# Two half heads instead of one pair: exponentials of an attention kernel split between ScalarE and VectorE

## The chip, the cores and the metric

One core of one Trainium2 chip. The metric is the device time of one execution in microseconds (us), the median of the runs shown. Lower is better.

## The reference, cut to what matters

Two attention layers over 2048 tokens of width 576 with 32 heads of 18 channels each; their outputs stand side by side. A has one key and one value head for all query heads (softmax over all 2048 keys). B has its own keys and values per head, works in four segments of 512 tokens with a causal mask, and adds a memory of the earlier segments.

```python
def _A_ref(x, wq, wk, wv, wo):
    q = (x @ wq).reshape(B, S, H, Dh).transpose(0, 2, 1, 3)
    k, v = x @ wk, x @ wv
    p = _softmax(jnp.einsum("bhqd,bkd->bhqk", q, k) * (Dh ** -0.5), axis=-1)
    return jnp.einsum("bhqk,bkd->bhqd", p, v) ... @ wo

def _B_ref(x, wq, wk, wv, wo, beta):
    for s in range(N):
        p = _softmax(jnp.einsum("bhqd,bhkd->bhqk", qs, ks) * scale + mask, axis=-1)
        a_dot = jnp.einsum("bhqk,bhkd->bhqd", p, vs)
        o = g * a_mem + (1.0 - g) * a_dot
    ...
return jnp.concatenate([a, b], axis=-1)
```

## The kernel before

**Stages.** The first 290 us or so project x into queries, keys and values and write them to DRAM. Then comes one long loop, written out by hand, that makes scores, exponentials and products of A and B; a short tail of some 40 us projects the last chunks of A. The change is in the loop.

**Blocks, items and turns.** A block of A is a chunk of 512 queries (c, 0 to 3) and a group of four heads (hg, 0 to 7), so there are 32 of them; a block of B is a segment and a group of heads. B's 32 blocks go two at a time between blocks of A. A block of A has 16 key tiles (kt) with two pairs of heads (pr) each. One item is one key tile and one pair: a score tile E of 128 keys x (2 heads x 512 queries). The 32 items of a block are taken three at a time, as ten turns of three and an eleventh of two; they are called turn 0 to turn 10 of the block here. A block of B has six items, in two turns.

**What a turn does**, in this program order:

- `scores` (L903 and on): TensorE writes the three score tiles E into PSUM, which has three such buffers (`psE`, two banks each).
- The middle item (`copied`, i == 1) is copied by VectorE from PSUM to a tile W in SBUF (L933); with that its buffer is free.
- ScalarE takes the exponential of the three (L936), first of items 0 and 2 straight from E, then of the middle one from W, into tiles P.
- `run_fill`: four matmuls of an output projection that is ready (L773), so that TensorE has work; at its fifth step VectorE copies the result out (osb, L797).
- `products` of the turn two before (L966), six halves of items cut into turns of their own by the list `prods`. Each half serves the four heads of the group, in fp32; in the trace an entry of three halves shows as 24 matmuls, one of two as 16. The entry of two, the short turn of products, stands third from the end of a block's entries, so it is made in the block's turn 10. When a block ends, VectorE copies its sums O out (oe, L975).
- `due`: steps from a list with due turns: loads, the inverses of the softmax sums (reciprocals, L729), and the weighing of the heads by them on GpSimd (`weigh`, L754 to L764, instructions of L761). Weighing steps cost 1 each and at most two are given out in a turn, none near a B turn (`heavy`).

TensorE, ScalarE and VectorE keep this order exactly; GpSimd keeps the order of its weighing steps among each other.

**VectorE's own exponential.** One item of each block of A, key tile 0 of pair 1 (`BY_DVE = ((0, 1),)`), is not given to ScalarE. It is item 1 of turn 0, so the middle one. `exponentials` (L888) reads its E once (a scaled integer form, L894) into a tile PD of 128 x 1024, and then six further steps on SBUF tiles follow, one each in turns 0, 2, 3, 4, 5 and 6: two bitwise ones (L896, L897) and four that multiply a polynomial (L898 to L901, `scalar_tensor_tensor` with two tensor inputs). A step's due turn is the turn of the scores plus two and more, but a step goes out as soon as no block ends in the turn; so each but the first in a block goes out a turn before it is due. `LATE = (12,)` puts the products with PD at position 12 of that pair's key tiles.

Of the kernel before, what the change touches and what calls it, by code (L numbers as in the profile page):

```python
# [8 lines left out]
F32 = mybir.dt.float32  # L9
# [3 lines left out]
U32 = mybir.dt.uint32  # L13
AF = mybir.ActivationFunctionType
# [14 lines left out]
SCALE = DH ** -0.5  # L29
# [3 lines left out]
PBUFS = 9  # L33
# [18 lines left out]
POLY = [1.0925606709321247, 32.334180715292455, 88.7610992882796, 4291.093056129828]  # L52
MANTISSA, ONE_BITS, EXPONENT = 0x7FFFFF, 0x3F800000, 0xFF800000

BY_DVE = ((0, 1),)
LATE = (12,)
QALL = [(slice(0, 36, 2), 0), (slice(1, 36, 2), 1), (slice(36, 54), 0)]
CA = 618
MZ = 126 + 32
# [15 lines left out]
def attention_pair_kernel(ctx, tc, a_xT, a_w, a_wo, b_xT, b_w, b_wo, b_beta, ident_d, hmask_d, bmask_d, cmask_d, sel_d, zmask_d, selx_d, sely_d, out):  # L75
    nc = tc.nc
# [79 lines left out]
    with ExitStack() as ph:  # L156
# [106 lines left out]
        for c in range(NCH):  # L263
# [34 lines left out]
            for t in TILES:  # L298
# [3 lines left out]
                else:  # L302

                    nm, bufs = ("nd", 2) if c == 1 and t == 4 else ("pj", 4)
# [25 lines left out]
                i = 5 * (c - 2) + TILES.index(t)  # L330
# [74 lines left out]
        for s in range(NSEG):  # L405
# [110 lines left out]
            if not last:  # L516
                e = p2.tile([128, 4, DH], F32, name="ph31")
# [92 lines left out]
    with tc.If(loose > 0, preferred_fallthrough_block=False):  # L610
        with ExitStack() as ph:
# [37 lines left out]
            with tc.For_i(0, H, 1) as h:  # L649
# [5 lines left out]
                for i in range(NKT):  # L655
                    s, j = divmod(i, 4)
                    n = 128 * (j + 1)
# [17 lines left out]
    pp = ctx.enter_context(tc.tile_pool(name="pp", bufs=1))  # L675
# [79 lines left out]
    def weigh(ab, c, t, tiles):  # L755

        o, (rb, *mem) = parts[ab, c][: RT[t], t], [x[: RT[t]] for x in tiles]

        def step(dst, a, b, op):

            return lambda: tc.keep_in_program_order(nc.gpsimd.tensor_tensor(dst, a, b, op=op))  # L761

        steps = [step(o, o, rb, ALU.mult)]
        if mem:  # L764
            nb, rb2 = mem
            steps += [step(nb, nb, rb2, ALU.mult), step(o, o, nb, ALU.add)]
        return steps
# [117 lines left out]
        vseg[s] = v  # L885


    slow, now = [], [0]  # L888

    def exponentials(p, e):  # L890

        y, u, w = p.bitcast(U32), pp.tile([128, 2, 512], F32, name="n", bufs=1), pp.tile([128, 2, 512], F32, name="q", bufs=1)
        v, stt = nc.vector, nc.vector.scalar_tensor_tensor
        v.tensor_scalar(y, e, EXP_A, EXP_B, op0=ALU.mult, op1=ALU.add)  # L894
        steps = [
            lambda: v.tensor_scalar(u.bitcast(U32), y, MANTISSA, ONE_BITS, op0=ALU.bitwise_and, op1=ALU.bitwise_or),  # L896
            lambda: v.tensor_scalar(w.bitcast(U32), y, EXPONENT, None, op0=ALU.bitwise_and),  # L897
            lambda: stt(p, u, POLY[0], u, op0=ALU.add, op1=ALU.mult),  # L898
            lambda: stt(p, p, POLY[1], u, op0=ALU.add, op1=ALU.mult),
            lambda: stt(p, p, POLY[2], p, op0=ALU.add, op1=ALU.mult),  # L900
            lambda: stt(p, p, POLY[3], w, op0=ALU.add, op1=ALU.mult),  # L901
        ]
        slow.extend((now[0] + 2 + i, p, step) for i, step in enumerate(steps))  # L903

    def scores(it, pr, copied):

        ab, c, hg, kt = it
        st = stacks[ab, c, hg // 2]
        h = 2 * (hg % 2) + pr
        e = psE.tile([128, 2, 512], F32, name="E")  # L910
        dve = ab == "A" and (kt, pr) in BY_DVE
        p = pp.tile([128, 2, 512], F32, name="PD" if dve else "P", bufs=1 if dve else PBUFS)
        state[it, pr] = p
        n = 512 if ab == "A" else 512 - 128 * kt if kt < 2 else 384
        if ab == "A":
            for j, r0 in enumerate(HALF):
                rows = slice(r0, r0 + KR)
                nc.tensor.matmul(e[:, j], kstA[rows, 128 * kt : 128 * kt + 128], st[rows, h, :], start=True, stop=True)  # L918
            if (kt, pr) in BY_DVE:
                exponentials(p, e)  # L920
                return lambda: None
        else:
            for k, c0 in BKEYS[kt]:
                ks = slice(128 * k, 128 * k + 128)
                for j, r0 in enumerate(HALF):
                    rows = slice(r0, r0 + KR)
                    nc.tensor.matmul(  # L927
                        e[:, j, c0 : c0 + 512 - 128 * k], st[rows, 4 + h, ks], st[rows, h, 128 * k :], start=True, stop=True
                    )
        src = e  # L930
        if copied:
            src = pp.tile([128, 2, 512], F32, name="W", bufs=2)
            nc.vector.tensor_copy(src[:, :, :n], e[:, :, :n])  # L933

        def exponential():
            nc.scalar.activation(p[:, :, :n], src[:, :, :n], AF.Exp, scale=SCALE)  # L936
            if ab == "B":

                m = len(BKEYS[kt])
                diag = p.rearrange("p a (b t) -> p a b t", t=256)[:, :, 0:m, 0:128]  # L940
                nc.gpsimd.affine_select(  # L941
                    diag, diag, pattern=[[0, 2], [0, m], [1, 128]], base=0, channel_multiplier=-1, compare_op=ALU.is_ge, fill=0.0
                )

        return exponential
# [3 lines left out]
    def products(b, m, hf):  # L949


        ab, c, hg = b
        if m == hf == 0:
            acc[0] = psO.tile([128, C], F32, name="O")
        o = acc[0]
        last = (NKT - 1 if ab == "A" else 2) == m
        for j in range(4):
            kt = turn_of[j // 2][m] if ab == "A" else m
            p = state[b + (kt,), j // 2]
            assert all(x[1] is not p for x in slow)  # L960
            k, p0, q0, n = (kt, 256 * hf, 256 * hf, 256) if ab == "A" else BHALF[kt][hf]
            if ab == "A":
                v = VA[:, VW * kt : VW * kt + 32]
            else:
                v = vseg[c][:, k, VW * (4 * hg + j) : VW * (4 * hg + j) + 32]
            nc.tensor.matmul(  # L966
                o[32 * j : 32 * j + 32, q0 : q0 + n],
                v,
                p[:, j % 2, p0 : p0 + n],
                start=m == hf == 0,  # L970
                stop=last and hf == 1,
            )
        if last and hf:
            osb = pa.tile([128, C], F32, name="oe", bufs=4)
            nc.vector.tensor_copy(osb, o)  # L975
            od = oA if ab == "A" else oB
            nc.sync.dma_start(od[c][4 * hg : 4 * hg + 4].rearrange("h r t -> (h r) t"), osb)
            return hg
        return None
# [27 lines left out]
    turns, prods = [], []  # L1007
# [5 lines left out]
    def due(k, most=2, heavy=2):  # L1013

        cost = 0

        near = [its[n][0] for t in turns[k : k + 3] for n, pr in t]
        heavy *= "B" not in near
        for e in [e for e in later if e[0] <= k]:
            if most and cost + e[1] <= heavy and e[2]():  # L1020
                later.remove(e)
                e[3](k)
                cost += e[1]
                most -= 1
        return cost
# [60 lines left out]
    with tc.manual_schedule(engines={ENG.PE, ENG.Activation, ENG.DVE}):  # L1086
# [3 lines left out]
        for n, b in enumerate(blocks):  # L1090
            ms = [m for m in range(len(its)) if block_of[m] == n]
            items = [(m, k) for m in ms for k in range(2)]
            for out_, cut in ((turns, len(items) // 3), (prods, len(items) // 3 - 2)):
                at_ = split(len(items), cut)
                out_ += [items[a:z] for a, z in zip(at_, at_[1:])]
        at(ASK + 4, 0, lambda: True, lambda k: load_qf(2))
# [13 lines left out]
        for k in range(len(turns) + 2):  # L1110
            now[0] = k
            exps = [scores(its[n], pr, i == 1) for i, (n, pr) in enumerate(turns[k])] if k < len(turns) else []
            for i in (0, 2, 1) if len(exps) == 3 else range(len(exps)):
                exps[i]()
            if memory is None:
                run_fill()
            elif k >= ASK and all(its[n][0] == "A" for n, pr in turns[k]) and next(memory, None) is None:
                memory = None

            ends = k > 1 and any(hf and its[n][3] == (NKT - 1 if its[n][0] == "A" else 2) for n, hf in prods[k - 2])  # L1120
            if slow and (slow[0][0] <= k or not ends):
                slow.pop(0)[2]()
            for n, hf in prods[k - 2] if k > 1 else []:
                ab, c = its[n][:2]
                hg = products(its[n][:3], its[n][3], hf)
                if hg in (6, 7):
                    finish(k, ab, c, hg)
                if hg == 7 and ab == "B" and c + 1 < NSEG:
                    load_vseg(c + 1)
            due(k)  # L1130
            if k == len(turns):
                halve_w(0)
            for n, pr in turns[k] if k < len(turns) else []:
                it = its[n]
                ab = it[0]
                if pr == 0:
                    prefetch(ab, keys[ab].index((ab, it[1], it[2] // 2)) + 2)
                    if it in (("A", 0, 2, 8), ("A", 0, 5, 8)):
                        load_wo(*(("B", b_wo) if it[2] == 2 else ("A", a_wo)))
# [122 lines left out]
```

## Time and profile before

| | us |
|---|---|
| median of 3 runs (lowest to highest) | 1421.66 (1420.84 to 1422.12) |
| profiled execution: time / its span | 1422.47 / 1420.7 |
| busy in the span: TensorE matmul / weight load | 1404.0 / 843.3 |
| busy in the span: ScalarE / VectorE / GpSimd | 1205.4 / 964.4 / 244.6 |
| granted TensorE clock, mean | 0.997 |

Instructions of one engine overlap in the profile: a ScalarE or VectorE instruction starts before the one ahead of it has ended, so durations can't be added up. What an engine needs for an instruction is read from end to end of successive ones. Matmuls overlap in the same way; their rate is read from start to start.

### The profile page before, as it was taken

What the parts mean: (1) busy time and instruction counts of PE and PEld (TensorE: products, weight loads), DVE (VectorE), ACT (ScalarE), POOL (GpSimd) and SP (SyncE); (2) the same over time, 40 slices, a digit from 0 to 9 for tenths busy, and PEclk for the clock granted to TensorE, in tenths of its full rate; (3) what the DMA queues carried; (4) which work ended last, traced back from release to release, by engine and by line L of the source; (5) the groups of instructions that cost most, each with busy time, mean ns of one, the idle gap of its engine ahead of it and who ended that gap; (6) DMA issues with size and microseconds to landing.
All of it is one profiled execution on the core that took longest, in us unless ns stands there. A gap on an engine that the chain in (4) does not pass through costs nothing.

```text
span 1420.7 us, 39951 instructions
## 1 busy us (share of the span) xinstructions
PE 1404.0 (99%) x17132; PEld 843.3 (59%) x17132; DVE 964.4 (68%) x1157; ACT 1205.4 (85%) x1447; POOL 244.6 (17%) x326
## 2 busy tenths in 40 slices
PE   9999999999999999999999999999999999999998
PEld 6788888745555555555555555555555555555558
DVE  6656456456677767776766777666767766777663
ACT  4543434479999999999999999999999999999991
POOL 2431000003313213221110160131011400100002
PEclk9999999999999999999999999999999999999999
DMA  9766546557564535332312543232104221110013
GB/s 283 253 216 188 166 146 214 174 171 214 156 214 159 165 120 166 91 109 77 110 58 70 166 128 92 62 107 80 51 34 132 67 76 44 60 45 18 9 59 112
DMA packets 90720, 172.63 MB, mean 122 GB/s; under 512 B 14576, under 2 KB 22889, under 8 KB 90110
## 3 DMA queue, kind: packets, MB, share of 16 engines
q1 hardware_dynamic: 84122, 160.01, 36.0%
q0 software_dynamic: 1664, 4.78, 1.3%
q10 hardware_dynamic: 4752, 5.24, 1.1%
q8 instruction: 135, 2.21, 0.7%
q14 instruction: 47, 0.39, 0.1%
HBM read 99.32 MB, written 70.67 MB: 120 GB/s over the span
## 4 chain that ended last, share of the span: by engine, by line
PE 68%; ACT 7%; issue 2%; DMA 1%; DVE 1%; SPq 0%; ACTq 0%; DVEq 0%
PE O L966 31%; PE E L918 20%; PE F L773 11%; ACT P L936 7%; PE E L927 3%; PE E L1163 2%; PE F L829 1%; DMA stB<-qB 0%; DVE W L933 0%; PE F L1163 0%; PE O L1163 0%; DMA oA<-oe 0%; DMA stB<-kB 0%; DMA sm<-oA 0%; SPq L696 0%
## 5 line engine op out<-in xcount | busy, mean ns | idle before, releaser
L936 ACT ACTIVATE P<-E 128x1024 f32<-128x1024 f32 (+1 forms) x800 | 780.8, 1059 | 12.7 <-PE E L918 12.3
L933 DVE COPY W<-E 128x1024 f32<-128x1024 f32 (+1 forms) x384 | 461.2, 1201 | 248.8 <-PE E L918 189.2
L966 PE MATMUL O<-P,VA 128*32 128x256 f32 x7936 | 508.8, 380 | 0.0
L936 ACT ACTIVATE P<-W 128x1024 f32<-128x1024 f32 (+1 forms) x384 | 426.3, 1110 | 3.4 <-DVE W L933 3.2
L966 PEld LDWEIGHTS O<-P,VA 128*32 128x32 f32 x7936 | 262.2, 110 | 147.6 <-issue 6.6
L918 PE MATMUL E<-stA,kstA 56*128 56x512 f32 x1920 | 329.4, 439 | 1.8 <-DVE W L933 1.1
L918 PEld LDWEIGHTS E<-stA,kstA 56*128 56x128 f32 x1920 | 154.7, 184 | 178.2 <-ACT P L936 113.7
L941 POOL TENSOR_SCALAR_AFFINE_SELECT P<-P 128x256 f32<-128x256 f32 (+1 forms) x192 | 95.0, 495 | 480.3 <-ACT P L936 446.9
L761 POOL TENSOR_TENSOR o<-o,rb 126x512 f32<-126x512 f32 (+1 forms) x55 | 79.9, 1468 | 408.9 <-DMA o<-oA 146.0
L773 PE MATMUL F<-woB,o 126*32 126x192 f32 (+1 forms) x1920 | 127.4, 338 | 0.3 <-DVE osb L797 0.3
L966 PE MATMUL O<-P,vseg 128*32 128x256 f32 (+2 forms) x1536 | 81.8, 344 | 0.8 <-issue 0.8
L773 PEld LDWEIGHTS F<-woB,o 126*32 126x32 f32 (+1 forms) x1920 | 38.2, 108 | 70.6 <-issue 63.6
L975 DVE COPY oe<-O 128x512 f32<-128x512 f32 x64 | 44.3, 692 | 41.8 <-PE O L966 41.0
L252 PE MATMUL pj<-xh,wBl 128*126 128x512 f32 x180 | 72.4, 403 | 0.0
L252 PE MATMUL pj<-xh,wBh 128*126 128x512 f32 x180 | 71.9, 400 | 0.0
L121 ACT CAST qp<-pj 126x512 fp32r<-126x512 f32 (+1 forms) x54 | 31.0, 585 | 46.1 <-DVE kmB L450 32.4
L966 PEld LDWEIGHTS O<-P,vseg 128*32 128x32 f32 x1536 | 49.1, 109 | 25.4 <-issue 2.9
L773 PE MATMUL F<-woA,o 126*32 126x192 f32 (+1 forms) x960 | 63.9, 338 | 0.0
L927 PE MATMUL E<-stB 56*128 56x256 f32 (+3 forms) x512 | 61.3, 347 | 1.4 <-ACT P L936 0.9
L122 DVE TENSOR_TENSOR qp<-pj,qp 126x512 fp32r<-126x512 f32 (+1 forms) x54 | 36.7, 685 | 35.6 <-ACT qp L121 35.3
L252 PE MATMUL pj<-xl,wBh 128*126 128x512 f32 x144 | 57.3, 399 | 0.0
L927 PEld LDWEIGHTS E<-stB 56*128 56x128 f32 x512 | 38.6, 185 | 31.1 <-ACT P L936 20.8
(194 smaller groups left out, 1387.8 us busy)
## 6 DMA issues: line engine op xcount, KB each, us to landing
stB<-kB SPq DMA_DIRECT2D x96, 144.0 KB
stB<-qB SPq DMA_DIRECT2D x32, 288.0 KB
stA<-qA SPq DMA_DIRECT2D x30, 288.0 KB
oA<-oe SPq DMA_DIRECT2D x32, 256.0 KB
oB<-oe SPq DMA_DIRECT2D x32, 256.0 KB
qA<-qp SPq DMA_DIRECT2D x16, 504.0 KB
kB<-qp SPq DMA_DIRECT2D x16, 504.0 KB
qB<-qp SPq DMA_DIRECT2D x16, 504.0 KB
```

Source lines behind the costliest of these rows:

```text
L121: hold(nc.scalar.copy(qp[:R, 0, :n], src))
L122: hold(nc.vector.tensor_tensor(qp[:R, 1, :n], src, qp[:R, 0, :n].bitcast(F32), op=ALU.subtract))
L252: nc.tensor.matmul(dst, w[:, c0 : c0 + M], x, start=i == 0, stop=i == len(ops) - 1)
L761: return lambda: tc.keep_in_program_order(nc.gpsimd.tensor_tensor(dst, a, b, op=op))
L773: nc.tensor.matmul(dst[32 * j : 32 * j + 32], parts[ab, c][: RT[t], t, r0 : r0 + 32], wo[ab][: RT[t], t, c0 : c0 + n], start=start, stop=stop,
L918: nc.tensor.matmul(e[:, j], kstA[rows, 128 * kt : 128 * kt + 128], st[rows, h, :], start=True, stop=True)
L927: nc.tensor.matmul(e[:, j, c0 : c0 + 512 - 128 * k], st[rows, 4 + h, ks], st[rows, h, 128 * k :], start=True, stop=True)
L933: nc.vector.tensor_copy(src[:, :, :n], e[:, :, :n])
L936: nc.scalar.activation(p[:, :, :n], src[:, :, :n], AF.Exp, scale=SCALE)
L941: nc.gpsimd.affine_select(diag, diag, pattern=[[0, 2], [0, m], [1, 128]], base=0, channel_multiplier=-1, compare_op=ALU.is_ge, fill=0.0)
L966: nc.tensor.matmul(o[32 * j : 32 * j + 32, q0 : q0 + n], v, p[:, j % 2, p0 : p0 + n], start=m == hf == 0, stop=last and hf == 1,)
L975: nc.vector.tensor_copy(osb, o)
```

## The change

1. Two items per block are shared: key tile 0 of pair 1 (turn 0) and key tile 5 of pair 0 (turn 3), both the middle item of their turn. VectorE makes the exponentials of the first head only (128 x 512); it also copies the second head to W (128 x 512), and ScalarE takes the exponential of that half. The six further steps go in pairs, two of 128 x 512 in each of three turns. PD has two buffers.
2. The products' short turn stands second from the end of the block's entries instead of third, so it is made in the turn after the block's turn 10.
3. Weighing steps are not given out where a slow step is due in this turn or the next (`heavy`), and each weighing instruction is made to wait for the copy W of its turn (`gate`).

```diff
-BY_DVE = ((0, 1),)
-LATE = (12,)
+BY_DVE = ((0, 1), (5, 0))
+LATE = (7, 12)
...
-            return lambda: tc.keep_in_program_order(nc.gpsimd.tensor_tensor(dst, a, b, op=op))
+            def run():
+                ins = tc.keep_in_program_order(nc.gpsimd.tensor_tensor(dst, a, b, op=op))
+                if gate:
+                    tc.add_manual_dep(ins.ins, gate[-1].ins.name, AFTER, reason="beside the copies of this turn")
+
+            return run
...
-    def exponentials(p, e):
-
-        y, u, w = p.bitcast(U32), pp.tile([128, 2, 512], F32, name="n", bufs=1), pp.tile([128, 2, 512], F32, name="q", bufs=1)
-        v, stt = nc.vector, nc.vector.scalar_tensor_tensor
+    def exponentials(p, e, whole):
+
+        u, w = (pp.tile([128, 512], F32, name=nm, bufs=1) for nm in "nq")
+        v, stt, y = nc.vector, nc.vector.scalar_tensor_tensor, p.bitcast(U32)
         v.tensor_scalar(y, e, EXP_A, EXP_B, op0=ALU.mult, op1=ALU.add)
...
-        slow.extend((now[0] + 2 + i, p, step) for i, step in enumerate(steps))
+        slow.extend((now[0] + 2 + i, p, ops[2 * i : 2 * i + 2], whole) for i in range(3))
...
-        p = pp.tile([128, 2, 512], F32, name="PD" if dve else "P", bufs=1 if dve else PBUFS)
+        p = pp.tile([128, 2, 512], F32, name="PD" if dve else "P", bufs=2 if dve else PBUFS)
...
-            if (kt, pr) in BY_DVE:
-                exponentials(p, e)
-                return lambda: None
+            if dve:
+                exponentials(p[:, 0], e[:, 0], p)
...
+        src, hs = e, slice(0, 2)
         if copied:
             src = pp.tile([128, 2, 512], F32, name="W", bufs=2)
-            nc.vector.tensor_copy(src[:, :, :n], e[:, :, :n])
+            hs = slice(1, 2) if dve else slice(0, 2)
+            gate.append(nc.vector.tensor_copy(src[:, hs, :n], e[:, hs, :n]))
...
-            nc.scalar.activation(p[:, :, :n], src[:, :, :n], AF.Exp, scale=SCALE)
+            nc.scalar.activation(p[:, hs, :n], src[:, hs, :n], AF.Exp, scale=SCALE)
...
-        heavy *= "B" not in near
+        heavy *= "B" not in near and all(e[0] > k + 1 for e in slow)
...
-            for out_, cut in ((turns, len(items) // 3), (prods, len(items) // 3 - 2)):
+            for out_, cut in ((turns, len(items) // 3), (prods, len(items) // 3 - 1)):
...
             if slow and (slow[0][0] <= k or not ends):
-                slow.pop(0)[2]()
+                for op in slow.pop(0)[2]:
+                    op()
```

More of the change, by code (lines that the diff above doesn't have):

```diff
@@ L885, in load_vseg @@
         vseg[s] = v
-    slow, now = [], [0]
-    def exponentials(p, e):
-        y, u, w = p.bitcast(U32), pp.tile([128, 2, 512], F32, name="n", bufs=1), pp.tile([128, 2, 512], F32, name="q", bufs=1)
-        v, stt = nc.vector, nc.vector.scalar_tensor_tensor
+    slow, now, gate = [], [0], []
+    AFTER = mybir.DependencyInfo(mybir.DependencyClass.Sync, mybir.DependencyReason.SCHED_ONLY)
+    def exponentials(p, e, whole):
+        u, w = (pp.tile([128, 512], F32, name=nm, bufs=1) for nm in "nq")
+        v, stt, y = nc.vector, nc.vector.scalar_tensor_tensor, p.bitcast(U32)
         v.tensor_scalar(y, e, EXP_A, EXP_B, op0=ALU.mult, op1=ALU.add)
-        steps = [
+        ops = [
             lambda: v.tensor_scalar(u.bitcast(U32), y, MANTISSA, ONE_BITS, op0=ALU.bitwise_and, op1=ALU.bitwise_or),
@@ L929, in scores @@
                     )
-        src = e
+        src, hs = e, slice(0, 2)
         if copied:
             src = pp.tile([128, 2, 512], F32, name="W", bufs=2)
-            nc.vector.tensor_copy(src[:, :, :n], e[:, :, :n])
+            hs = slice(1, 2) if dve else slice(0, 2)
+            gate.append(nc.vector.tensor_copy(src[:, hs, :n], e[:, hs, :n]))
         def exponential():
-            nc.scalar.activation(p[:, :, :n], src[:, :, :n], AF.Exp, scale=SCALE)
+            nc.scalar.activation(p[:, hs, :n], src[:, hs, :n], AF.Exp, scale=SCALE)
             if ab == "B":
@@ L959, in products @@
             p = state[b + (kt,), j // 2]
-            assert all(x[1] is not p for x in slow)
+            assert all(x[3] is not p for x in slow)
             k, p0, q0, n = (kt, 256 * hf, 256 * hf, 256) if ab == "A" else BHALF[kt][hf]
```

## The prediction

> **What bounds the kernel now.** First the busy times, then who waits for whom.
>
> ```profile
> PE 1404.0 (99%) x17132; PEld 843.3 (59%) x17132; DVE 964.4 (68%) x1157; ACT 1205.4 (85%) x1447; POOL 244.6 (17%) x326
> ACT  4543434479999999999999999999999999999991
> ACT P L936 <- PE E L918: 12.3, 31, 1.8
> ACT P L936 <- DVE W L933: 3.2, 8, 0.9
> PEld E L918 <- ACT P L936: 124.5, 348, 1.1
> ```
>
> The page and the list of waits are read together. In the loop (slices 9 to 39) ScalarE is never free for long. It waits 31 times for a score, about once per block of A, and 8 times for a copy W. TensorE, busy at 99% because matmuls overlap, waits 348 times for ScalarE to free a score buffer. So ScalarE sets the pace, and TensorE is close behind. The timeline of ScalarE gives the sizes: a block that follows A (first three rows: turn 10's last, turn 0, turn 1), one that follows B (next five), and a stretch of B.
>
> ```profile
> 573.28 1.10 ACT L936 ACTIVATE P<-W 128x1024 f32<-128x1024 f32 x1
> 574.23 1.98 ACT L936 ACTIVATE P<-E 128x1024 f32<-128x1024 f32 x2
> 576.46 1.94 ACT L936 ACTIVATE P<-E 128x1024 f32<-128x1024 f32 x2 [0.24 <-PE E L918]
> ...
> 913.33 1.94 ACT L936 ACTIVATE P<-E 128x1024 f32<-128x1024 f32 x2
> 915.82 1.94 ACT L936 ACTIVATE P<-E 128x1024 f32<-128x1024 f32 x2 [0.55 <-PE E L918]
> 917.64 1.06 ACT L936 ACTIVATE P<-W 128x1024 f32<-128x1024 f32 x1
> 918.59 1.94 ACT L936 ACTIVATE P<-E 128x1024 f32<-128x1024 f32 x2
> 920.40 1.08 ACT L936 ACTIVATE P<-W 128x1024 f32<-128x1024 f32 x1
> ...
> 905.34 1.24 ACT L936 ACTIVATE P<-W 128x1024 f32<-128x1024 f32 x1
> 906.29 1.69 ACT L936 ACTIVATE P<-E 128x768 f32<-128x768 f32 x2
> 907.67 1.04 ACT L936 ACTIVATE P<-W 128x768 f32<-128x768 f32 x1
> ```
>
> From end to end: two from E take 1.83 (574.38 to 576.21), one from W 0.94 (917.76 to 918.70), so a turn takes 2.77. At 768 columns W takes 0.73 (907.98 to 908.71) and E 0.70. 256 columns are thus 0.21, and a half W of 512 comes to 0.52.
>
> Turn 0 has only two exponentials, 1.83, and TensorE can't keep up: turn 1 begins 2.19 - 1.83 = 0.36 late behind A and 2.49 - 1.83 = 0.66 late behind B. Read so at all 32 starts of turn 1: 0.34 to 0.36 at seventeen, 0.56 to 0.67 at ten, 0.33 at two, nothing at three; in sum 13.0. That is what could be won there; elsewhere ScalarE has no gap to lose.
>
> **Sharing two items.** Per block ScalarE gives up one more whole W (0.945) and takes two halves (1.04): +0.095, in 32 blocks +3.0. Of this, 0.52 falls into turn 0, where ScalarE waited. Behind A the 0.36 vanish; behind B 0.66 - 0.52 = 0.14 stay. Won: 17 x 0.35 + 2 x 0.33 + 10 x 0.52 = 11.8. Net -8.8, if TensorE and VectorE follow.
>
> **TensorE and the short turn.** Rows of a block that follows A, from turn 0 on, then the scores of two full turns.
>
> ```profile
> 573.05 1.18 PE L918 MATMUL E<-stA,kstA 56*128 56x512 f32 x6
> 574.51 1.48 PE L966 MATMUL O<-P,VA 128*32 128x256 f32 x24
> 575.92 0.96 PE L918 MATMUL E<-stA,kstA 56*128 56x512 f32 x6
> 577.16 1.05 PE L966 MATMUL O<-P,VA 128*32 128x256 f32 x16
> ...
> 920.26 0.96 PE L918 MATMUL E<-stA,kstA 56*128 56x512 f32 x6
> 922.92 0.97 PE L918 MATMUL E<-stA,kstA 56*128 56x512 f32 x6
> ```
>
> A full turn costs TensorE 2.66; eight product matmuls 0.43. The short turn of products leaves turn 10 for the turn behind it. Scores of turn 0 then begin at 573.48 instead of 573.05, still ahead of the end of W at 574.38, and take 0.96 instead of 1.18 because their buffer is free by then; 0.43 less follows, so turn 1's scores begin at 575.70 instead of 575.92. Cost nothing, hidden under ScalarE; without that cover 0.43 a block, 14. With ScalarE's own start later by 0.16, turn 1's scores are 0.38 earlier against their use. Turn 3 takes ScalarE 1.83 + 0.52 = 2.35 but TensorE 2.66: it eats 0.31 of a lead that is 0.38 at turn 1 and grows by 2.77 - 2.66, some 0.12, each turn. Enough, by 0.3.
>
> **VectorE.** Its cover is the time between the end of a copy and the moment ScalarE needs W.
>
> ```profile
> 914.76 0.69 DVE L896 TENSOR_SCALAR n<-PD 128x1024 uint32<-128x1024 uint32 x1
> 916.12 1.22 DVE L933 COPY W<-E 128x1024 f32<-128x1024 f32 x1 [0.67 <-PE E L918]
> 922.25 1.22 DVE L898 SCALAR_TENSOR_TENSOR PD<-n 128x1024 f32<-128x1024 f32 x1
> 923.77 1.23 DVE L933 COPY W<-E 128x1024 f32<-128x1024 f32 x1 [0.31 <-PE E L918]
> 1076.71 1.75 DVE L729 RECIPROCAL sm<-sm 112x256 f32<-112x256 f32 x1
> 1078.69 1.22 DVE L933 COPY W<-E 128x1024 f32<-128x1024 f32 x1
> ...
> 925.91 1.12 ACT L936 ACTIVATE P<-W 128x1024 f32<-128x1024 f32 x1
> 1079.94 1.06 ACT L936 ACTIVATE P<-W 128x1024 f32<-128x1024 f32 x1 [0.28 <-DVE W L933]
> ...
> L975 DVE COPY oe<-O 128x512 f32<-128x512 f32 x64 | 44.3, 692 | 41.8 <-PE O L966 41.0
> ```
>
> At 1079.94 W was late: from the copy's end (1079.91) to the exponential's end (1081.00) are 1.09, no cover. In turn 1 (916.12, W at 917.64) it is 1.36 - 1.09 = 0.27, in turn 4 (923.77, W at 925.91) 0.94. In the new kernel, with the lead above: behind A 0.65, 0.77, then 0.39 in turn 3 and 0.59, 0.71, 0.83 in turns 4 to 6; behind B 0.27, 0.71, 0.33, 0.53, 0.65, 0.77.
>
> A step of 512 takes 0.69 by L975 (same width), a bitwise one 0.42 (the CAST below). Copies overlap neighbours by 0.08, a dependent step starts 0.03 later: copy to copy 0.61 + 0.72 - 0.08 + 1.22 = 2.47 in a step turn, under 2.77. Turn 3, with two halves of 0.69, is 0.07 longer there. Undisturbed: nothing. The reciprocal behind turn 6's steps meets a pair 0.19 longer and, in blocks behind B, a cover of 0.77 instead of 1.10: +0.5 each in three blocks and 0.4 in a fourth, +1.9.
>
> **Weighing.** The new condition on `heavy` does nothing. At `due` the step of this turn has gone out, and since steps run one turn early, the next is due at k + 2, never at k + 1. Followed through the code, the weighing steps fall in the same turns as before: of 65 in the loop 31 in turns with steps. No DMA moves, on SP or POOL. But each now waits for its turn's copy, and behind the copy come VectorE's steps. Before, GpSimd ran as soon as its loads had landed (568.19 below), turns ahead of that. What a meeting costs, VectorE rows first, then GpSimd's:
>
> ```profile
> 47.99 0.41 DVE L208 CAST xh<-xr 128x512 fp32r<-128x512 f32 x1
> 48.44 1.96 DVE L214 TENSOR_TENSOR xl<-xr,xh 128x512 fp32r<-128x512 f32 x1
> 16.97 0.69 DVE L214 TENSOR_TENSOR xl<-wBl,xh 128x512 fp32r<-128x512 f32 x1
> 17.58 0.42 DVE L208 CAST xh<-wBl 128x512 fp32r<-128x512 f32 x1
> ...
> 48.01 1.84 POOL L243 TENSOR_TENSOR wBl<-wr,wBh 128x648 fp32r<-128x648 f32 x1 [19.30 <-DMA xr<-a_xT]
> 50.75 1.60 POOL L243 TENSOR_TENSOR wBl<-wr,wBh 128x648 fp32r<-128x648 f32 x1
> 17.14 1.80 POOL L214 TENSOR_TENSOR xl<-wBl,xh 128x512 fp32r<-128x512 f32 x1 [16.09 <-DVE xh L208]
> 568.19 1.29 POOL L761 TENSOR_TENSOR o<-o,rb 126x512 f32<-126x512 f32 x1 [0.30 <-DMA rb<-rB]
> ```
>
> At 48.01 GpSimd waited for the CAST, came in the 0.03 before the dependent subtraction, and that took 1.96 instead of 0.69: +1.27, for a GpSimd step of 1.60. For one of 1.29 the delay lies between 0.96 and 1.27; I take 1.1. A polynomial pair is dependent in the same way. At 17.14 GpSimd also waited, but the CAST at 17.58, independent of what ran, kept its 0.42. The bitwise pair (turns 0, 4) is independent: I take 0, bound 1.1.
>
> The ledger: copy to copy becomes 3.57 in a turn with polynomial steps and weighing, cover changes by 2.77 - 3.57 = -0.80; a bitwise turn gives it back. In three blocks (hg 7 of c 0, 1, 2) weighing stands in turns 3, 4, 5, 6. Starting from 0.39 at turn 3, W is 0.41 late at turn 4, has a cover of 0.95 at turn 5 (2.77 less the 1.82 of a bitwise turn) and 0.15 at turn 6, and is 0.65 late at turn 7; with a result copy (osb) now and then 1.25 a block. In three (hg 6) it stands in turns 5 and 6: from 0.71, 0.09 late and then 0.80, with osb some 1.0. Two more blocks some 0.5 each. Sum 7.75. The meetings of before, some 0.9 of the 3.2 above, go: net +6.9. Behind the waiting GpSimd stand only further weighing and, turns later, B's masks; the projection that uses the heads starts two turns on: nothing.
>
> The Trainium skill, "SBUF — State Buffer", section "Who interferes with whom", says that a VectorE instruction with two SBUF inputs and a GpSimd one that reads SBUF exclude each other, and the first to issue holds the ports for its whole length. Row 48.44 agrees (1.96). Row 17.58 doesn't: GpSimd had issued 0.44 earlier.
>
> **Sum.** -8.8 + 1.9 + 6.9 = 0.0 on the profiled 1422.47, which is 0.8 above the median 1421.66. Forecast: no change, 1421.6; measurable is 0.2%, 2.8 us.
>
> **Rivals.** (1) GpSimd doesn't get between dependent steps in the loop, or covers hold it: -8.8 + 1.9 - 0.9 = -7.8, 1413.9. For it: only eight late W in all of before. Against: row 48.44. (2) Slower: the ports also go to GpSimd between the bitwise pair, at 1.27 each time. It decides in turn 4 of the three hg 7 blocks, where the cover then isn't won back: 3 x 1.1, and 0.17 at nine late meetings: +4.9, 1426.5. For it 48.44, against it 17.58. The skill's rule of first issue would make just this happen. (3) TensorE's lead doesn't carry turn 3, 0.31 in each of the 29 blocks whose turn 1 waited: +9.0, 1430.6. Against: buffer waits of 124.5 us. (4) That the weighing is kept out as said would bring rival 1's time; the code excludes it.
>
> **Numbers.** Forecast 0.45 (1418.8 to 1424.5 its own range), rival 1 0.27, rival 2 0.20, rival 3 0.08. Range 1413.5 to 1427.5: it holds rivals 1 and 2 and leaves out 3 and the tails. Faster: most of rival 1 and a small part of the forecast, 0.33; within 0.2% 0.40; slower, most of 2, 3 and a part, 0.27.
>
> **What would show it.** ScalarE's waits for scores at turn 1 fall from 13 to some 1.3; turn 3 takes 2.35 from end to end; its waits for W grow to some 10, in the hg 6 and hg 7 blocks; second steps of pairs under weighing take 1.8. Wrong if W isn't late there, or turn 4 begins with a wait for scores.

## The result and the profile after

The changed kernel takes 1423.36 us in the median of 14 runs (1422.17 to 1424.75), the kernel before 1420.88 in 14 runs beside them (1419.23 to 1423.55). The ratio is 1.0019, with a 95% interval of 1.0012 to 1.0027: slower by some 2.5 us. The profiled execution took 1422.96 with a span of 1421.2.

The busy times, then the waits of ScalarE and of TensorE's weight loads on ScalarE and VectorE (idle us in sum, times, and the longest), answer to the first rows of the prediction. The kernel's lines have moved by six: the scores are L924, the copy W L939, the exponential L942, the products L972.

```profile
PE 1400.0 (99%) x17132; PEld 843.1 (59%) x17132; DVE 997.0 (70%) x1413; ACT 1208.7 (85%) x1479; POOL 239.6 (17%) x326
...
ACT P L942 <- DVE W L939: 11.2, 20, 1.0
ACT P L942 <- PE E L924: 2.4, 3, 1.9
...
PEld E L924 <- ACT P L942: 90.2, 249, 1.1
PEld E L924 <- DVE W L939: 13.0, 22, 0.8
```

ScalarE's wait has changed its releaser. It waited 12.3 us for scores (E) and 3.2 for copies (W); now it is 2.4 and 11.2. VectorE is 33 us busier. The next rows are ScalarE's timeline for a block that follows A, from the last turn of the block before it to turn 6.

```profile
573.98 1.08 ACT L942 ACTIVATE P<-W 128x1024 f32<-128x1024 f32 x1
574.93 1.97 ACT L942 ACTIVATE P<-E 128x1024 f32<-128x1024 f32 x2
576.73 0.67 ACT L942 ACTIVATE PD<-W 128x512 f32<-128x512 f32 x1
577.25 1.98 ACT L942 ACTIVATE P<-E 128x1024 f32<-128x1024 f32 x2
...
582.77 2.02 ACT L942 ACTIVATE P<-E 128x1024 f32<-128x1024 f32 x2
584.58 0.73 ACT L942 ACTIVATE PD<-W 128x512 f32<-128x512 f32 x1
585.10 2.04 ACT L942 ACTIVATE P<-E 128x1024 f32<-128x1024 f32 x2
587.30 1.06 ACT L942 ACTIVATE P<-W 128x1024 f32<-128x1024 f32 x1 [0.17 <-DVE W L939]
588.27 1.92 ACT L942 ACTIVATE P<-E 128x1024 f32<-128x1024 f32 x2
590.42 1.06 ACT L942 ACTIVATE P<-W 128x1024 f32<-128x1024 f32 x1 [0.23 <-DVE W L939]
591.39 1.92 ACT L942 ACTIVATE P<-E 128x1024 f32<-128x1024 f32 x2
593.85 1.06 ACT L942 ACTIVATE P<-W 128x1024 f32<-128x1024 f32 x1 [0.55 <-DVE W L939]
```

Turn 0 (574.93 and 576.73) now has a half W, and turn 1 (577.25) begins without a wait. The late copies stand in turns 4, 5 and 6 instead, one behind the other. Why they are late is seen on VectorE in another block with much weighing (c 1, hg 7), turns 3 to 5; GpSimd's rows stand behind.

```profile
855.79 0.68 DVE L906 SCALAR_TENSOR_TENSOR PD<-PD 128x512 f32<-128x512 f32 x1
856.51 1.66 DVE L907 SCALAR_TENSOR_TENSOR PD<-PD,q 128x512 f32<-128x512 f32 x1
858.09 1.21 DVE L939 COPY W<-E 128x1024 f32<-128x1024 f32 x1
859.23 0.41 DVE L902 TENSOR_SCALAR n<-PD 128x512 uint32<-128x512 uint32 x1
859.56 1.51 DVE L903 TENSOR_SCALAR q<-PD 128x512 uint32<-128x512 uint32 x1
860.99 1.21 DVE L939 COPY W<-E 128x1024 f32<-128x1024 f32 x1
862.12 0.68 DVE L904 SCALAR_TENSOR_TENSOR PD<-n 128x512 f32<-128x512 f32 x1
862.83 1.67 DVE L905 SCALAR_TENSOR_TENSOR PD<-PD,n 128x512 f32<-128x512 f32 x1
```
```profile
855.95 1.67 POOL L762 TENSOR_TENSOR o<-o,rb 126x512 f32<-126x512 f32 x1 [8.85 <-DVE W L939]
859.38 1.40 POOL L762 TENSOR_TENSOR rb<-rb 126x512 f32<-126x512 f32 x1 [1.76 <-DVE W L939]
862.34 3.29 POOL L762 TENSOR_TENSOR o<-o,rb 126x512 f32<-126x512 f32 x2 [1.56 <-DVE W L939]
```

Each weighing instruction is released by a copy and begins just behind it, beside the first step of the pair. By the rows it waits that step out and runs before the second: GpSimd's row of 855.95 ends at 857.62, and the second step, which began at 856.51, ends 0.55 after that. The second step of a polynomial pair takes 1.66 or 1.67 instead of the undisturbed 0.69, so 0.97 more; and the second bitwise step (859.56) takes 1.51 instead of 0.41, so 1.10 more, though its first step (859.23) gives it nothing. There is no idle time between copies in these turns.

### The profile page after: what moved, and what is told of

It reads as the page before. It is cut to its first block, busy times and chain, and to the rows that moved or that the text cites. A ratio compares the mean times of both kernels' runs of the same rounds, so it can differ in the third digit from the quotient of the medians.

```text
span 1421.2 us, 40402 instructions
## 1 busy us (share of the span) xinstructions
PE 1400.0 (99%) x17132; PEld 843.1 (59%) x17132; DVE 997.0 (70%) x1413; ACT 1208.7 (85%) x1479; POOL 239.6 (17%) x326
## 4 chain that ended last, share of the span: by engine, by line
PE 65%; DVE 6%; ACT 4%; issue 3%; DMA 1%; POOL 0%; SPq 0%; DVEq 0%; ACTq 0%
PE O L972 30%; PE E L924 19%; PE F L778 10%; ACT P L942 4%; PE E L932 3%; DVE W L939 3%; PE E L1170 2%; PE F L834 1%; DVE PD L906 1%; DVE PD L904 1%; DMA vseg<-vB 1%; DVE sm L729 0%; DVE PD L905 0%; DMA woA<-a_wo 0%; PE F L1170 0%
## 5 line engine op out<-in xcount | busy, mean ns | idle before, releaser
L942 ACT ACTIVATE P<-E 128x1024 f32<-128x1024 f32 (+1 forms) x800 | 793.0, 1088 | 2.6 <-PE E L924 2.4
L939 DVE COPY W<-E 128x1024 f32<-128x1024 f32 (+2 forms) x416 | 465.3, 1119 | 206.5 <-PE E L924 145.0
L972 PE MATMUL O<-P,VA 128*32 128x256 f32 x7680 | 508.2, 380 | 0.0
L942 ACT ACTIVATE P<-W 128x1024 f32<-128x1024 f32 (+1 forms) x352 | 400.0, 1136 | 11.2 <-DVE W L939 11.2
L972 PEld LDWEIGHTS O<-P,VA 128*32 128x32 f32 x7680 | 260.4, 110 | 138.5 <-issue 5.6
L924 PE MATMUL E<-stA,kstA 56*128 56x512 f32 x1920 | 324.6, 435 | 7.8 <-DVE W L939 6.8
L924 PEld LDWEIGHTS E<-stA,kstA 56*128 56x128 f32 x1920 | 155.0, 184 | 176.0 <-ACT P L942 78.9
L972 PE MATMUL O<-P,vseg 128*32 128x256 f32 (+2 forms) x1536 | 81.4, 344 | 0.0
L972 PE MATMUL O<-PD,VA 128*32 128x256 f32 x512 | 71.7, 379 | 0.0
L972 PEld LDWEIGHTS O<-P,vseg 128*32 128x32 f32 x1536 | 48.8, 109 | 24.4 <-issue 1.8
L900 DVE TENSOR_SCALAR PD<-E 128x512 uint32<-128x512 f32 x64 | 44.2, 691 | 27.0 <-PE E L924 26.2
```

The source lines that it names most:

```text
L939: gate.append(nc.vector.tensor_copy(src[:, hs, :n], e[:, hs, :n]))
L942: nc.scalar.activation(p[:, hs, :n], src[:, hs, :n], AF.Exp, scale=SCALE)
L972: nc.tensor.matmul(o[32 * j : 32 * j + 32, q0 : q0 + n], v, p[:, j % 2, p0 : p0 + n], start=m == hf == 0, stop=last and hf == 1,)
```

## The experiments

The theory after the result: ScalarE's gain of turn 1 is there, and is lost again to copies that come late because weighing parts every pair of steps, the bitwise one too. Its rivals: that the wait given to the weighing is the cost by itself; that the short turn of products or the halves cost more than was reckoned. Kernels of the first four experiments ran beside the kernel before at 1420.82 us, the last three at 1421.18.

**Without the wait.**

```diff
                 ins = tc.keep_in_program_order(nc.gpsimd.tensor_tensor(dst, a, b, op=op))
-                if gate:
-                    tc.add_manual_dep(ins.ins, gate[-1].ins.name, AFTER, reason="beside the copies of this turn")
```

> The change without the wait of the weighing for its turn's copy; all else as changed. Theory (the wait puts GpSimd's steps behind the copy, where VectorE's pairs of steps stand): GpSimd runs ahead again, the late W of the hg 6 and hg 7 blocks shrink from 8.3 us to some 2, and the time falls by 6 to 8 us against the changed kernel, some 5 us under the kernel before (ratio near 0.996). Rival (the halves themselves, or VectorE's longer work in the step turns, cost it): the time stays within 2 us of the changed kernel, above the kernel before.

Measured: 1427.11 us (1421.49 to 1431.03), ratio 1.0045 (1.0031 to 1.0059). The theory's number is missed, and with the wrong sign: it is slower than the change. VectorE's rows of turns 3 to 4 of a block, and GpSimd's:

```profile
827.76 1.43 DVE L904 SCALAR_TENSOR_TENSOR PD<-PD 128x512 f32<-128x512 f32 x1
829.22 1.66 DVE L905 SCALAR_TENSOR_TENSOR PD<-PD,q 128x512 f32<-128x512 f32 x1
...
832.28 1.51 DVE L901 TENSOR_SCALAR q<-PD 128x512 uint32<-128x512 uint32 x1
```
```profile
826.09 2.55 POOL L762 TENSOR_TENSOR o<-o,rb 126x512 f32<-126x512 f32 x2 [3.46 <-DMA rb<-rB]
828.60 3.42 POOL L762 TENSOR_TENSOR rb<-rb 126x512 f32<-126x512 f32 x2
831.98 4.68 POOL L762 TENSOR_TENSOR o<-o,rb 126x512 f32<-126x512 f32 x3
```

Without the wait GpSimd runs several weighings in one go from the moment a load lands (826.09), and then both steps of a pair are hit, 1.43 and 1.66. So the wait is not what costs: by the medians the kernel without it is 3.7 slower than the changed one, outside the rival's 2 us too. What the slower runs lost is not seen, since the profiled execution took 1423.59, and ScalarE's waits for whole copies in it come to 12.0 us, 11.2 in the changed kernel. That GpSimd's place now hangs on landings would account for the runs' spread, 9.5 us against 2.6 of the changed kernel; that link is argued, not shown.

**The kernel before with the wait alone.**

```diff
-            return lambda: tc.keep_in_program_order(nc.gpsimd.tensor_tensor(dst, a, b, op=op))
+            def run():
+                ins = tc.keep_in_program_order(nc.gpsimd.tensor_tensor(dst, a, b, op=op))
+                if gate:
+                    tc.add_manual_dep(ins.ins, gate[-1].ins.name, AFTER, reason="beside the copies of this turn")
+
+            return run
...
-            nc.vector.tensor_copy(src[:, :, :n], e[:, :, :n])
+            gate.append(nc.vector.tensor_copy(src[:, :, :n], e[:, :, :n]))
```

> The kernel before with the wait alone added. Theory (a single step of 1024 per turn already holds the ports when the weighing is released, so GpSimd waits and then runs beside the next copy; only a second step in the same turn is hit): no change, -1 to +1 us. Rival (the wait as such costs, whatever stands behind the copy): slower by 4 us or more, with late W in the hg 6 and hg 7 blocks.

Measured: 1421.13 us, ratio 1.0005 (0.9997 to 1.0014): no change, as the theory had it. With one whole step in a turn, GpSimd (second fence) waits it out and then runs beside the next copy, which isn't longer for it:

```profile
582.86 1.22 DVE L904 SCALAR_TENSOR_TENSOR PD<-n 128x1024 f32<-128x1024 f32 x1
584.37 1.23 DVE L939 COPY W<-E 128x1024 f32<-128x1024 f32 x1 [0.29 <-PE E L924]
```
```profile
583.02 2.21 POOL L762 TENSOR_TENSOR o<-o,rb 126x512 f32<-126x512 f32 x1 [8.81 <-DVE W L939]
```

**Weighing kept out of step turns.** The change's condition is replaced by one that bites.

```diff
-        heavy *= "B" not in near and all(e[0] > k + 1 for e in slow)
+        heavy *= "B" not in near and stepped[0] != k
...
                 for op in slow.pop(0)[2]:
                     op()
+                stepped[0] = k
```

> The change with a condition that does keep the weighing out of turns in which a step went out; the wait stays. Theory: the late W of the hg 6, hg 7 and two further blocks (10.5 us) vanish, the reciprocals stay; the projections start some turns later and leave about three more of their steps for the tail (1.4 us). About 8 us faster than the changed kernel, 5 to 6 us faster than the kernel before (ratio near 0.996). Rival (halves cost it): no gain over the changed kernel.

Measured: 1416.17 us, ratio 0.9968 (0.9959 to 0.9978): 7.2 under the changed kernel and 4.7 under the kernel before, each somewhat less than expected. ScalarE's waits in its profile:

```profile
ACT P L942 <- DVE W L939: 5.6, 6, 1.8
ACT P L942 <- PE E L924: 3.1, 4, 2.0
```

Six late whole copies are left of twenty. The weighing that is put off is paid for in part behind the loop: from the loop's last exponential to the end of the span it is 42.68 us, in the changed kernel 40.83.

**The wait moved behind the pair.** Weighing stays in its turns, but waits for the turn's last step instead of its copy.

```diff
                 for op in slow.pop(0)[2]:
-                    op()
+                    last = op()
+                gate.append(last)
```

> The change, with the weighing waiting for the last step of its turn where there is one, instead of the copy: as many waits, in the same turns, a place further. Theory: GpSimd then runs beside the next copy; only the second weighing step of turn 5 in the three hg 7 blocks still meets a pair, about 1 us each. 5 to 7 us faster than the changed kernel, 3 to 4 under the kernel before. Rival (any wait of GpSimd for VectorE costs as much): as the changed kernel.

Measured: 1414.52 us, ratio 0.9957 (0.9944 to 0.9970): 8.8 less than the changed kernel by the two medians, more than the 5 to 7 expected. The same block as above (c 1, hg 7), first VectorE, then GpSimd:

```profile
854.59 0.69 DVE L907 SCALAR_TENSOR_TENSOR PD<-PD,q 128x512 f32<-128x512 f32 x1
855.25 1.22 DVE L939 COPY W<-E 128x1024 f32<-128x1024 f32 x1
```
```profile
855.36 1.28 POOL L762 TENSOR_TENSOR o<-o,rb 126x512 f32<-126x512 f32 x1 [10.16 <-DVE PD L907]
```

The pair keeps 0.69, GpSimd runs beside the copy out of PSUM, and the copy takes 1.22. It is the same amount of weighing in the same turns: only what it lies beside has changed. In the six hg 6 and hg 7 blocks no copy is late any more, where 8.3 us were lost in the changed kernel. So the collision with the pairs is the cause of the loss.

**Weighing kept out of the two bitwise turns only.** This takes away the term that the forecast put at nothing.

```diff
-        heavy *= "B" not in near and all(e[0] > k + 1 for e in slow)
+        heavy *= "B" not in near and stepped[0] != k
...
+                bits = slow[0][4] == 0
                 for op in slow.pop(0)[2]:
                     op()
+                if bits:
+                    stepped[0] = k
```

> The change with the weighing kept out of the turns with the two bitwise steps alone (turns 0 and 4); it goes a turn further, into turns with polynomial steps. Theory (GpSimd takes the ports in the bitwise turn too, so W can't catch up there): in the three hg 7 blocks W is no longer late at turns 5 and 6 (2.6 us in sum), the late W of turns 4 and 7 stay; 2 to 3 us faster than the changed kernel, level with the kernel before (ratio 0.999 to 1.001). Rival (the prediction's: a bitwise pair is never parted): nothing changes, or it gets worse since turn 6 has one weighing step more.

Measured: 1421.95 us, ratio 1.0000 (0.9991 to 1.0009): level with the kernel before, as expected, but only 1.4 under the changed kernel by the medians (2 to 3 expected). Turn 4 of block c 1, hg 7:

```profile
859.46 0.41 DVE L902 TENSOR_SCALAR n<-PD 128x512 uint32<-128x512 uint32 x1
859.79 0.41 DVE L903 TENSOR_SCALAR q<-PD 128x512 uint32<-128x512 uint32 x1
860.20 1.23 DVE L939 COPY W<-E 128x1024 f32<-128x1024 f32 x1
```

With 0.41 twice, copies in the three hg 7 blocks are late at turn 4 (0.28, 0.42, 0.65) and turn 7 (0.61, 0.43, 0.44), and no more at turns 5 and 6: 2.8 us in sum, 5.9 in the changed kernel. That is the course that the prediction wrote down for these blocks (0.41 and 0.65). The time of the whole kernel tests it less well, though it is the time forecast: elsewhere copies came later, at turns 3 and 4 of c 2, hg 2 by 1.3 us instead of 0.6.

**The short turn put back.**

```diff
-(prods, len(items) // 3 - 1)
+(prods, len(items) // 3 - 2)
```

> The change with the products' short turn where it was before. Theory (TensorE's work in turns 10 and 0 together is the same, only a buffer wait of 0.2 comes back): starts of turn 1 behind A still don't wait, or by less than 0.1; 0 to 2 us slower than the changed kernel. Rival (the shift is what makes the shared turn 0 possible): some 0.2 to 0.4 at each of 17 starts of turn 1, 4 to 7 us slower.

Measured: 1424.44 us, ratio 1.0023 (1.0013 to 1.0032), 1.1 above the changed kernel's median (0.8 when each is taken against the kernel before that ran beside it). ScalarE's wait for scores is the same:

```profile
ACT P L942 <- PE E L924: 2.3, 3, 1.7
```

The halves alone take the wait of turn 1 away; moving the short turn brings a microsecond at most, and the two intervals overlap.

**Wait behind the pair, and reciprocals out of step turns.** The wait as in the fourth experiment, and with it:

```diff
-            at(k + d1, 0, lambda: True, inv)
+            at(k + d1, 0, lambda: last or stepped[0] != now[0], inv)
...
+                stepped[0] = k
```

> The change with the weighing behind the turn's last step, and the reciprocals given out only in turns without a step (but for the last chunk). Theory: the late W at turn 7 behind the reciprocals (0.8 to 1.2 in four blocks, 3.9 in sum) fall to 0.3 or less each; 3 us faster than with the weighing behind the steps alone, near 1411.5 (ratio 0.9935). Rival (those late W are made up elsewhere): as that kernel.

Measured: 1411.87 us (1409.97 to 1413.26), ratio 0.9930 (0.9915 to 0.9944). It is near the 1411.5 expected and under both kernels. The late copies at turn 7 behind the reciprocals, 3.9 us in the fourth experiment, are gone; one of 0.4 at turn 10 (c 0, hg 2) is new. Its span, busy times and ScalarE's waits:

```profile
span 1408.7 us, 40390 instructions
...
PE 1393.8 (99%) x17132; PEld 843.2 (60%) x17132; DVE 976.2 (69%) x1413; ACT 1206.2 (86%) x1479; POOL 231.6 (16%) x326
...
ACT P L942 <- PE E L924: 1.9, 2, 1.7
ACT P L942 <- DVE W L939: 1.7, 4, 0.8
```

VectorE is 20.8 us less busy than in the changed kernel with the same 1413 instructions. Nearly all of it, 20.2, is in the steps of the exponentials (L902 to L907), 23 of which took over 0.9 us in the changed kernel and two here.

## Why the prediction was wrong

The forecast was no change, 1421.6; it is slower by 2.5, inside the range and by the way of rival 2, at about half its price. Times below are read as in the prediction, from end to end of ScalarE's instructions, over all 32 blocks of A. A copy is late by what its exponential takes over the undisturbed 0.946 (0.518 for a half).

- **Turn 1: right.** The 13.06 of lateness at its starts are 1.37 now; 11.8 were to be won, 11.7 were.
- **Two halves: right.** A half W takes ScalarE 0.518 (0.52 forecast); 2 x 0.518 - 0.946 in 32 blocks is +2.9 (forecast +3.0).
- **The short turn and turn 3: right.** Turn 3 takes 2.35 from end to end (582.96 to 585.31), and turn 4 does not begin with a wait for scores, but for one block (c 0, hg 2: 0.34). Rival 3 falls. The short turn costs nothing; nor was its move needed, as the sixth experiment shows.
- **Reciprocals: right.** In their four blocks W was late by 1.73 in sum and is by 3.83: +2.1 (forecast +1.9). The next fence has VectorE's rows of one, and then ScalarE's.

```profile
1077.75 0.69 DVE L907 SCALAR_TENSOR_TENSOR PD<-PD,q 128x512 f32<-128x512 f32 x1
1078.36 1.74 DVE L729 RECIPROCAL sm<-sm 112x256 f32<-112x256 f32 x1
1080.14 0.29 DVE L732 TENSOR_SCALAR sm<-sm,omg 112x128 f32<-112x128 f32 x1
...
1081.59 1.06 ACT L942 ACTIVATE P<-W 128x1024 f32<-128x1024 f32 x1 [0.86 <-DVE W L939]
```

- **Weighing: this step failed.** It read "The bitwise pair (turns 0, 4) is independent: I take 0, bound 1.1". The pair costs 1.10 under a weighing (row 859.56). In the third hg 7 block (c 0), a result copy stands ahead of the pair, GpSimd comes before both, and the first step takes the delay instead (1.47). The cover of 0.95 that turn 5 was to have is then gone; the three blocks are late at turns 4, 5, 6 and 7, by 5.9 in sum instead of 3.75. With weighing out of the bitwise turns it is 2.8 (fifth experiment). The two blocks put at 0.5 each came to 2.2, the hg 6 blocks to 2.4 instead of 3.0. Together 10.5 instead of 7.75; less the meetings of before, 9.3 instead of 6.9. The bitwise pairs make 2.2 of the 2.4 between these; the rest came out at nearly nothing because its errors cancel, which is luck. One of them isn't weighing: 0.57 in c 0, hg 3 falls on the half W of turn 3, behind two VectorE steps of B's memory (L839 and L843, 0.74 and 0.70) that the forecast doesn't name, and it stays 0.59 in the third, fourth and seventh experiment.
- **The sum**, with what the runs showed: -11.7 + 2.9 + 2.1 + 10.5 - 1.2 (the meetings of before) = +2.6, measured +2.5. It holds only the terms that the forecast named.

How the step came to fail: the choice rested on one row of the start, 17.58, where a CAST kept its 0.42 while GpSimd had issued earlier and waited. The row shows a step that was not delayed; it doesn't show that independence was the reason. The profile of before held a row against it, two below the row 48.44 that the prediction goes by:

```profile
50.32 0.68 DVE L122 TENSOR_TENSOR qp<-pj,qp 126x512 fp32r<-126x512 f32 x1
50.92 1.72 DVE L208 CAST xh<-xr 128x512 fp32r<-128x512 f32 x1
```

This CAST has the form of the other and does not depend on the instruction ahead of it, yet it took 1.30 more than 0.42, behind GpSimd's row 50.75, which issued 0.17 before it. GpSimd was running there and not waiting, so the case isn't quite that of the loop, but it shows that independence alone doesn't guard a step.

The prediction had set its row against the Trainium skill, "SBUF — State Buffer", section "Who interferes with whom". What it quotes from there is said of VectorE instructions with two SBUF inputs; the CAST and the bitwise steps have one, so row 17.58 was no test of it. That the order of issue decides who waits, which that section of the Trainium skill says too, holds in the loop: at 859.38 GpSimd issues 0.18 ahead of the step at 859.56, and the step waits, though it doesn't depend on the one before. Why the CAST at 17.58 was spared stays open.

**The rivals.** Rival 1 (GpSimd doesn't get between) took its evidence from before's few late copies. That evidence doesn't carry: before had one step in a turn, so there was nothing to get between (second experiment). Rival 2 had mechanism and place right, but its +4.9 took 1.27 a time; it is 0.97 to 1.10, and without its 0.17 at nine meetings it would have been +3.3. Rival 4, that the weighing would be kept out as said, was rightly excluded by the code; the third experiment shows what that would have given, 1416.17.

**Two profiles, one difference.** That the sum meets the medians to 0.1 is in part luck, for it is read from two single executions, and these are only 0.5 apart (1422.47 and 1422.96). From the end of the loop's second exponential to the end of its last it is 1085.22 us before and 1086.58 after, 1.36 more. In the last block a copy late by 1.01 in the profile of before was late by 0.12 in that of after; the reciprocal ahead of it waits for a load, and the copy's lateness ranged from nothing to 1.96 over the profiles here. Without this copy the loop is 2.25 longer. What is left between that and the medians is not explained.

## What to carry to other kernels

Where a wait is to put a GpSimd instruction beside VectorE's copies, try releasing it from the last SBUF step ahead of the copy, not from the copy before: here the same weighing in the same turns cost 8.8 us less so. When work is cut into pairs of short instructions, ask what the other engine does in the seam, for dependent and independent pairs alike. And a slack that a later turn is to give back counts as gone until a row of that very turn shows it.

## What was unexpected of the hardware

In the loop a waiting GpSimd instruction parted two VectorE steps that don't depend on each other as it parted dependent ones: 1.51 instead of 0.41, beside 1.66 instead of 0.69. Its delay is nearly the same in both, 1.10 and 0.97, and shorter than its own 1.29. A copy from PSUM beside it keeps its 1.22.
